# Low weight words on VectorE, and two blocks of batch 0 accumulated high words first

## The chip, the cores and the metric

The kernel runs on one core of one Trainium2 chip. The metric is the device time of one execution in microseconds (us); the profile's "span" is the part of it from the first to the last instruction. Five engines work side by side, each through its own queue in order: TensorE (PE, matrix products), VectorE (DVE), ScalarE (ACT), GpSimd (POOL) and SyncE (SP, which issues the transfers).

## The reference, cut to what matters

Four batches of 1088 tokens go through a linear attention with a quadratic feature map and then a gated feed-forward block, in which a 1088 x 1088 matrix `w_sg` mixes the tokens:

```
x   = num / den                                  # attention: per batch 1088 x 128
h   = gelu(x @ w_in)                             # 1088 x 1024
u, v = h[..., :512], h[..., 512:]
v_n = (v - mean(v)) / sqrt(var(v) + 1e-6) * g_ln # over the 512 columns
v_s = w_sg @ v_n + b_sg                          # over the tokens, per batch
out = x + (u * v_s) @ w_out
```

The mixing product is by far the largest: 1088 x 1088 x 512 in each of four batches.

## The kernel before, in words

**Two words for a number.** TensorE multiplies a reduced form of float32 (`F32R`) in one pass. To keep the precision, an operand is split into a high word (the value rounded to F32R, by a cast on ScalarE) and a low word (value minus high word, a subtraction). A product is then the sum of three: high by high, high by low, low by high. So `w_sg` is held as `w_h` (one tile, nine row blocks) and as nine tiles `w_l0` to `w_l8`; the normalized v as `vh` and `vl`.

**Tiling.** Tokens are nine row blocks (`NT`; the last has 64 rows), or three column chunks (`CH`: 364, 362, 362). The 512 columns of v and u are four blocks of 128 (`NB`, index `db`). One unit of the mixing product is a pair (`db`, `ci`): a PSUM bank `pz` of 128 x 364 takes 26 products, for each row block t `w_h` by `vh`, `w_h` by `vl` (not in the last block, whose lower half holds the low word) and `w_l` by `vh`. Names in the rows carry the batch: `pz0_1_2` is batch 0, block 1, chunk 2.

**Stages of one batch.** Attention gives x as `x_h`, `x_l`. Nine tiles `pv` (`v1`, three products each) give v before the gelu; `gelu` on ScalarE, `stats` on VectorE, then `norm`, a chain of twelve tiny VectorE instructions that gives the reciprocal root `rs` and `nm` for a group of row blocks (batch 0: blocks 0-1, 2-4, 5-8). `v3` applies them, `split_h` and `split_l` make `vh` and `vl`. `unit` (tile `pu`) makes u before its gelu (`ug`); it needs the two words of the first half of `w_in`, which VectorE converts from 64-bit floats (`wi0`, tiles `win_h`, `win_l`). `scale` and `gate` (tile `gt`) empty a `pz` bank, and three products (`po`) with `w_out` add to the output.

**What sets the order.** Each step is registered with `at(name, f)`; the table `WHEN` gives every step its rank, and the steps are issued in that order. Each engine runs its own steps in that order and waits for semaphores. PSUM has eight banks, handed out in turn: a step that takes a bank waits until its last reader is done.

**Around the change.** Batch 0 is special, since its weights have only just arrived. `w_hi` (ScalarE cast) and `w_lo` (subtraction) make the words of `w_sg`; `LO_POOL` names all nine low words, so GpSimd subtracts them. The mixing product of block 0 is done in two phases, all `w_h` products of the three chunks (`z_hi`) and then all `w_l` products (`z_lo`); blocks 1 to 3 go chunk by chunk through `main(g0, 1)`, with the three products of a row block side by side.

Of the kernel before, what the change touches and what calls it, by code (L numbers as in the profile page):

```python
# [8 lines left out]
I32 = mybir.dt.int32  # L9
# [7 lines left out]
NT = 9  # L17
# [121 lines left out]
def tile_kernel(tc, qd, kd, vd, sd, wd, bd, wind, gd, woutd, identd, outd, pool, dram, psum):  # L139
# [483 lines left out]
    def w_lo(t, E):  # L623
        T["w_l", t] = w = new([P, S], "w", f"w_l{t}", F32R)
        r = slice(0, P if t < NT - 1 else 64)
        if t == NT - 1:
            G.memset(f32(w[64:128]), 0.0)
        E.tensor_sub(w[r], T["w_f", t][r], f32(T["w_h"][r, t]))  # L628
# [350 lines left out]
```

## Time and profile before

| | |
|---|---|
| median of 3 runs | 373.79 us (373.56 to 376.94) |
| the profiled execution | 373.27 us, of which the span is 371.5 us |
| PE busy | 345.0 us, 93% of the span |
| DVE busy | 265.5 us, 71% |
| ACT busy | 165.9 us, 45% |
| POOL busy | 42.8 us, 12% |
| mean granted TensorE clock | 0.963 |

In the rows, `L628` is line 628 of the kernel as it was before; the changed kernel's lines stand one to three further. A row of the timeline gives start, duration, engine, line, operation, out<-in, shape and count, and in brackets how long the engine had been idle and what ended that. A row of the windows gives for each engine the busy us and the number of instructions in a stretch, then the granted TensorE clock, the share of the DMA engines and GB/s.

### The profile page before, as it was taken

Reading aid. Unit: us, or ns where it says so; the run is one execution under the profiler, and the core shown is the slowest. Engines: PE = TensorE matmul, PEld = TensorE weight load, DVE = VectorE, ACT = ScalarE, POOL = GpSimd, SP = SyncE. Lnnn points to the kernel's source line nnn. Section 1 sums busy time; section 2 is a strip of 40 time slices with the busy share of each in tenths; the row PEclk is TensorE's granted clock in tenths of the full one; section 3 lists DMA queues with packets and bytes.
Section 4 is the critical chain, followed back from the end, with each engine's and each line's share of the span. In section 5 each row is a group of like instructions: output and inputs, shape, how many; then the busy total and the mean of one; then the engine's idle time right before and its main releaser. Section 6 shows DMA issues by size and latency. Waiting matters only on the chain.

```text
span 371.5 us, 5469 instructions
## 1 busy us (share of the span) xinstructions
PE 345.0 (93%) x2040; PEld 329.7 (89%) x2040; DVE 265.5 (71%) x615; ACT 165.9 (45%) x361; POOL 42.8 (12%) x33
## 2 busy tenths in 40 slices
PE   8967059999989999999999999999999999999995
PEld 6866059999989999998989999999998999999994
DVE  5989997954897975655997984657999773535233
ACT  4737358524635591423565672334525861312020
POOL 0237930003200000013200000022200000000000
PEclk9969558999999999999999999999999999999999
DMA  7991020185200000176200010172000010000001
GB/s 256 377 394 60 0 84 2 26 179 164 77 0 20 2 20 23 35 159 202 50 2 20 3 40 2 38 173 66 0 2 1 2 40 2 0 20 2 0 2 60
DMA packets 13945, 24.17 MB, mean 65 GB/s; under 512 B 1856, under 2 KB 10720, under 8 KB 13920
## 3 DMA queue, kind: packets, MB, share of 16 engines
q1 hardware_dynamic: 13776, 23.75, 21.6%
q8 instruction: 16, 0.26, 0.3%
q10 hardware_dynamic: 144, 0.09, 0.1%
q14 instruction: 9, 0.07, 0.1%
HBM read 17.84 MB, written 2.65 MB: 55 GB/s over the span
## 4 chain that ended last, share of the span: by engine, by line
PE 63%; DVE 19%; DMA 8%; issue 3%; SPq 3%; ACT 2%; DVEq 0%; ACTq 0%
PE pz L725 15%; PE pz L731 15%; PE pz L727 13%; DVE den L472 3%; DMA e_2b<-e_2d 2%; SPq L434 2%; DMA e_2d<-ab 2%; PE po L794 2%; PE pu L745 2%; PE pu L746 2%; PE pu L747 2%; PE po L792 2%; PE po L793 2%; PE pv L653 2%; PE pv L655 1%
## 5 line engine op out<-in xcount | busy, mean ns | idle before, releaser
L725 PE MATMUL pz<-w_h,vh 128*128 128x362 f32 (+1 forms) x432 | 144.9, 335 | 4.1 <-ACT vh L707 3.1
L731 PE MATMUL pz<-w_l,vh 128*128 128x362 f32 (+1 forms) x432 | 137.6, 328 | 0.0
L727 PE MATMUL pz<-w_h,vl 128*128 128x362 f32 (+1 forms) x384 | 126.9, 331 | 0.0
L725 PEld LDWEIGHTS pz<-w_h,vh 128*128 128x128 f32 x432 | 82.4, 191 | 5.3 <-ACT vh L707 3.6
L731 PEld LDWEIGHTS pz<-w_l,vh 128*128 128x128 f32 x432 | 80.6, 188 | 0.0
L727 PEld LDWEIGHTS pz<-w_h,vl 128*128 128x128 f32 x384 | 73.3, 191 | 0.6 <-DVE vl L715 0.3
L757 DVE SCALAR_TENSOR_TENSOR gt<-pz,g_col,b_bc 128x362 f32<-128x362 f32 (+1 forms) x48 | 28.3, 591 | 40.2 <-PE pz L731 40.0
L768 ACT CAST gh<-gt 128x362 fp32r<-128x362 f32 (+1 forms) x47 | 23.1, 494 | 47.4 <-DVE gt L763 37.1
L752 ACT ACTIVATE u<-pu 128x362 f32<-128x362 f32 (+1 forms) x48 | 22.6, 471 | 45.9 <-PE pu L747 31.8
L771 DVE TENSOR_TENSOR gl<-gt,gh 128x362 fp32r<-128x362 f32 (+1 forms) x47 | 25.8, 552 | 12.0 <-ACT gh L768 11.2
L697 ACT ACTIVATE vn<-vn,nm,rs 128x512 f32<-128x512 f32 x36 | 27.9, 809 | 9.1 <-DVE nm L689 9.1
L707 ACT CAST vh<-vn 128x128 fp32r<-128x128 f32 (+1 forms) x72 | 25.5, 402 | 13.3 <-PE pz L731 12.9
L715 DVE TENSOR_TENSOR vl<-vn,vh 128x128 fp32r<-128x128 f32 (+2 forms) x68 | 26.0, 410 | 6.4 <-ACT vh L707 6.0
L763 DVE TENSOR_TENSOR gt<-gt,u 128x362 f32<-128x362 f32 (+1 forms) x48 | 25.5, 533 | 4.4 <-ACT u L752 3.4
L663 DVE BATCH_NORM_STATS2 st<-vn 128x6 f32<-128x512 f32 x36 | 24.4, 677 | 2.5 <-ACT vn L659 2.4
L628 POOL TENSOR_TENSOR w_l<-w_f,w_h 128x1088 fp32r<-128x1088 f32 (+1 forms) x9 | 23.2, 2574 | 24.3 <-ACT w_h L621 18.2
L659 ACT ACTIVATE vn<-pv 128x512 f32<-128x512 f32 x36 | 20.8, 599 | 10.1 <-PE pv L655 7.8
L451 POOL TENSOR_TENSOR qpl<-e_0a,qph 128x364 fp32r<-128x364 f32 x6 | 6.5, 1090 | 160.3 <-ACT qph L446 125.6
L746 PE MATMUL pu<-x_h,win_l 128*128 128x362 f32 (+1 forms) x48 | 16.6, 346 | 7.9 <-DVE win_l L230 7.9
L472 DVE RECIPROCAL den<-den 128x362 f32<-128x362 f32 (+1 forms) x9 | 21.7, 2415 | 2.2 <-ACT den L467 2.2
L745 PE MATMUL pu<-x_h,win_h 128*128 128x362 f32 (+1 forms) x48 | 16.8, 351 | 3.5 <-ACT win_h L228 3.5
L191 DVE TENSOR_TENSOR kp<-pk,kb 128x256 f32<-128x256 f32 x27 | 10.9, 420 | 8.6 <-ACT kb L354 6.3
(173 smaller groups left out, 507.7 us busy)
## 6 DMA issues: line engine op xcount, KB each, us to landing
w_f<-in_w SPq DMA_DIRECT2D x9, 544.0 KB, 8.3
vx<-in_v SPq DMA_DIRECT2D x8, 288.0 KB, 3.8
k<-in_k SPq DMA_DIRECT2D x3, 576.0 KB, 5.3
out<-o SPq DMA_DIRECT2D x7, 181.0 KB, 1.9
e_0a<-ab SPq DMA_DIRECT2D x6, 182.0 KB
e_0b<-e_0d SPq DMA_DIRECT2D x6, 182.0 KB
q<-in_q SPq DMA_DIRECT2D x6, 181.0 KB, 2.3
e_1a<-ab SPq DMA_DIRECT2D x6, 181.0 KB, 3.9
```

The source lines that it names most:

```text
L472: V.reciprocal(self.den[ci], self.den[ci])
L663: V.bn_stats(st, self.vn[:, t])
L697: A.activation(self.vn[:, t], self.vn[:, t], AF.Identity, bias=self.nm[:, t : t + 1], scale=self.rs[:, t : t + 1])
L707: A.copy(self.parts[db][0][:, ts], self.vn[:, ts, P * db : P * db + P])
L715: V.tensor_sub(vl[:, ts], vs[:, ts], f32(vh[:, ts]))
L725: mm(z, lhsT=vh[:, t], rhs=T["w_h"][:, t, cs], start=(t == 0), stop=False)
L727: mm(z, lhsT=vl[:, t], rhs=T["w_h"][:, t, cs], start=False, stop=False)
L731: mm(self.z[db, ci], lhsT=self.parts[db][0][:, t], rhs=T["w_l", t][:, c0 : c0 + cw], start=False, stop=(t == NT - 1),)
L745: mm(pu, lhsT=T["win_h"][:, ws], rhs=xh[:, cs], start=True, stop=False)
L757: V.scalar_tensor_tensor(gt, self.z.pop((db, ci)), T["g_col"][:, db : db + 1], T["b_bc"][:, c0 : c0 + cw], op0=ALU.mult, op1=ALU.add,)
L763: V.tensor_mul(self.gt[db, ci], self.gt[db, ci], self.u.pop((db, ci)))
L771: V.tensor_sub(self.g[db, ci][1], self.gt.pop((db, ci)), f32(self.g[db, ci][0]))
```

## The change

All nine low words of `w_sg` are subtracted on VectorE. In batch 0, blocks 0 and 1 (six `pz` banks) go through the two phases together: first the `w_h` products of all six, then the `w_l` products of all six. The u products (`pu`) of these blocks stand behind their `w_l` products in the list, each with its gelu. In `norm`, the shift and the multiply-add that start the reciprocal root are one instruction. And the table `WHEN` is a new one throughout, so that every engine's order differs in every batch.

```
@@ WHEN
-    0, 2, 3, 1, 4, 5, 6, 8, 12, 16, 21, 24, 27, 31, 35, 39, 44, 47, 50, 54, 59, 66, 79, 81, 34, 10, 11, 7, 13, 9,
+    0, 5, 2, 1, 3, 4, 6, 8, 12, 16, 21, 24, 26, 30, 32, 35, 40, 43, 47, 50, 54, 58, 68, 72, 41, 10, 11, 9, 13, 7,
...
-    def w_lo(t, E):
+    def w_lo(t):
...
-        E.tensor_sub(w[r], T["w_f", t][r], f32(T["w_h"][r, t]))
+        V.tensor_sub(w[r], T["w_f", t][r], f32(T["w_h"][r, t]))
...
-                lambda: V.tensor_scalar(yi(), w("v").bitcast(I32), 1, None, op0=ALU.logical_shift_right),
-                lambda: V.tensor_scalar(yi(), yi(), -1.0, float(0x9EF759DF), op0=ALU.mult, op1=ALU.add),
+                lambda: V.tensor_scalar(
+                    yi(), w("v").bitcast(I32), -0.5, float(0x1EF759DF), op0=ALU.mult, op1=ALU.add
+                ),
...
-    for ci in range(len(CH)):
-        at(("pu", 0, 0, ci), lambda ci=ci: g0.unit(0, ci))
+    def unit(g, db, ci):
+        at(("pu", g.b, db, ci), lambda: g.unit(db, ci))
+        at(("ug", g.b, db, ci), lambda: g.ug(db, ci))
+
+    for i in range(3):
+        split3(g0, 1, i)
+    for db in range(2):
+        for t in range(NT):
+            for ci in range(len(CH)):
+                at(("zh", 0, db, ci, t), lambda db=db, ci=ci, t=t: g0.z_hi(db, ci, t))
     for t in range(NT):
+        at(("wlo", t), lambda t=t: w_lo(t))
+    for db in range(2):
+        for t in range(NT):
+            for ci in range(len(CH)):
+                at(("zl", 0, db, ci, t), lambda db=db, ci=ci, t=t: g0.z_lo(db, ci, t))
         for ci in range(len(CH)):
-            at(("zh", 0, ci, t), lambda ci=ci, t=t: g0.z_hi(0, ci, t))
-    for t in range(NT):
-        at(("wlo", t), lambda t=t: w_lo(t, G if t in LO_POOL else V))
-        for ci in range(len(CH)):
-            at(("zl", 0, ci, t), lambda ci=ci, t=t: g0.z_lo(0, ci, t))
-    for ci in range(len(CH)):
-        gated(g0, 0, ci)
+            unit(g0, db, ci)
+            gated(g0, db, ci)
...
-    main(g0, 1)
+    main(g0, 2)
...
-LO_POOL = (0, 1, 2, 3, 4, 5, 6, 7, 8)
```

What the order means is seen in three places. The first is VectorE where batch 0's first norm group (tiles `nv0_0`, `ny0_0`, `nh0_0`) is worked out. Before:

```order
L680 TENSOR_SCALAR ny0_0_445<-ny0_0_445 128x2
L220 SCALAR_TENSOR_TENSOR wi0e_435<-wi0e_435,wi0g_447 128x512
L229 TENSOR_TENSOR wi0t_422<-wi0t_422,win_h_80 128x512
L681 TENSOR_TENSOR nh0_0_457<-ny0_0_445 128x2
L230 TENSOR_TENSOR win_l_82<-wi0t_422,wi0e_435 128x512
L682 TENSOR_TENSOR nh0_0_457<-nh0_0_457,nv0_0_442 128x2
```

In the changed kernel the same chain reads:

```order
L680 TENSOR_SCALAR ny0_0_406<-nv0_0_396 128x2
L664 BN_STATS st0_3_408<-vn0_143 128x6
L665 BN_AGGR mv0_364<-st0_3_408 128x2
L683 TENSOR_TENSOR nh0_0_416<-ny0_0_406 128x2
L664 BN_STATS st0_4_418<-vn0_143 128x6
L665 BN_AGGR mv0_364<-st0_4_418 128x2
L684 TENSOR_TENSOR nh0_0_416<-nh0_0_416,nv0_0_396 128x2
```

The conversion of the first half of `w_in` (`wi0t`, `wi0e`, `win_l`) no longer stands inside the chain; statistics of later row blocks (`BN_STATS`) do.

The second place is the low words. Before, they are a run on GpSimd:

```order
L628 TENSOR_TENSOR w_l3_432<-w_f3_181,w_h_79 128x1088
L628 TENSOR_TENSOR w_l4_450<-w_f4_186,w_h_79 128x1088
L628 TENSOR_TENSOR w_l6_484<-w_f6_202,w_h_79 128x1088
L628 TENSOR_TENSOR w_l7_518<-w_f7_215,w_h_79 128x1088
L627 MEMSET w_l8_566 64x1088
L628 TENSOR_TENSOR w_l8_566<-w_f8_226,w_h_79 64x1088
```

Now they stand on VectorE: two of them (`w_l1`, `w_l0`) ahead of the first `x_l`, and seven behind the last norm group, the end of which reads:

```order
L629 TENSOR_TENSOR w_l3_617<-w_f3_174,w_h_79 128x1088
L220 TENSOR_SCALAR wi0g_627<-wi0t_536 128x512
L629 TENSOR_TENSOR w_l7_631<-w_f7_199,w_h_79 128x1088
L230 TENSOR_TENSOR wi0t_536<-wi0t_536,win_h_80 128x512
L719 TENSOR_TENSOR vh0_0_458<-vn0_143,vh0_0_458 64x128
L629 TENSOR_TENSOR w_l6_647<-w_f6_192,w_h_79 128x1088
L629 TENSOR_TENSOR w_l8_656<-w_f8_209,w_h_79 64x1088
L221 SCALAR_TENSOR_TENSOR wi0e_581<-wi0e_581,wi0g_627 128x512
L231 TENSOR_TENSOR win_l_82<-wi0t_536,wi0e_581 128x512
```

The `wi0` conversion is threaded between them, and `win_l` of the first half comes last. The memset of `w_l8` is still GpSimd's; in the changed kernel that tile takes over the buffer that `w_l6` reads (`w_f6`), so the memset stands between the two subtractions.

The third place is TensorE where the mixing product of batch 0 begins. Before, behind two u tiles (`pu0_0_0`, `pu0_0_1`):

```order
L746 MATMUL pu0_0_1_476<-x0_h_333,win_l_82 128x362
L747 MATMUL pu0_0_1_476<-x0_l_334,win_h_80 128x362
L725 MATMUL pz0_0_2_507<-w_h_79,vh0_0_499 128x362
L727 MATMUL pz0_0_2_507<-w_h_79,vl0_0_500 128x362
L725 MATMUL pz0_0_1_514<-w_h_79,vh0_0_499 128x362
```

Now `pz` follows the last `pv` tile directly, and block 1 joins after twelve products:

```order
L727 MATMUL pz0_0_1_480<-w_h_79,vh0_0_458 128x362
L729 MATMUL pz0_0_1_480<-w_h_79,vl0_0_459 128x362
L727 MATMUL pz0_1_0_499<-w_h_79,vh0_1_486 128x364
L729 MATMUL pz0_1_0_499<-w_h_79,vl0_1_487 128x364
L727 MATMUL pz0_1_2_509<-w_h_79,vh0_1_486 128x362
L729 MATMUL pz0_1_2_509<-w_h_79,vl0_1_487 128x362
```

No u product stands ahead of the first `w_l` product any more: `pu0_0_0` comes behind 116 products of the mixing.

More of the change, by code (lines that the diff above doesn't have):

```diff
@@ L816, in gated @@
     def gated(g, db, ci):
-        at(("ug", g.b, db, ci), lambda: g.ug(db, ci))
         at(("gt", g.b, db, ci), lambda: g.scale(db, ci))
@@ L873, in main @@
             for ci in range(len(CH)):
-                at(("pu", g.b, db, ci), lambda db=db, ci=ci: g.unit(db, ci))
+                unit(g, db, ci)
                 for t in range(NT):
```

173 rows, old and new, of the table WHEN are left out of this document.

## The prediction

> **What bounds the kernel now.** First the busy shares, the slices and the granted clock on the page:
>
> ```profile
> PE 345.0 (93%) x2040; PEld 329.7 (89%) x2040; DVE 265.5 (71%) x615; ACT 165.9 (45%) x361; POOL 42.8 (12%) x33
> PE   8967059999989999999999999999999999999995
> POOL 0237930003200000013200000022200000000000
> PEclk9969558999999999999999999999999999999999
> ```
>
> TensorE is the bound from the seventh slice on. Before that it has a hole of three slices (9.3 us each), with the clock at half, and GpSimd is busiest just there. So the second view is the busy time by stage: the stretch and its length, then busy us and instructions of PE, PEld, DVE, ACT and POOL, the granted clock, the DMA share and GB/s:
>
> ```profile
> 35.10:52.10 17.00, 2.55 (x6) 1.69 (x6) 16.93 (x33) 7.07 (x11) 11.54 (x5) 0.59 0.09 31
> 52.10:58.70 6.60, 6.57 (x21) 6.24 (x22) 4.24 (x24) 4.13 (x8) 0.00 (x0) 0.50 0.11 40
> 58.70:110.00 51.30, 50.08 (x312) 48.44 (x311) 40.87 (x80) 25.73 (x63) 6.35 (x6) 1.00 0.33 81
> 110.00:371.50 261.50, 255.62 (x1523) 247.69 (x1522) 174.97 (x410) 110.05 (x249) 11.94 (x12) 1.00 0.13 35
> ```
>
> Between the last `pv` and the first `pz` TensorE works 2.55 of 17 us, while VectorE is full. From 58.7 on TensorE loses 1.2 us in 51, and 5.9 us in the rest, drain of the output included. The end is therefore the time at which TensorE gets going, plus a fixed amount of products. What fills VectorE in the hole is seen instruction by instruction, with GpSimd's below:
>
> ```profile
> 37.74 2.46 DVE L679 TENSOR_SCALAR ny<-nv 128x2 int32<-128x2 int32 x1
> 40.12 0.41 DVE L219 TENSOR_SCALAR wi0g<-wi0t 128x512 int32<-128x512 int32 x1
> 40.46 2.43 DVE L680 TENSOR_SCALAR ny<-ny 128x2 int32<-128x2 int32 x1
> 42.80 0.68 DVE L220 SCALAR_TENSOR_TENSOR wi0e<-wi0e,wi0g 128x512 f32<-128x512 int32 x1
> 43.41 2.96 DVE L229 TENSOR_TENSOR wi0t<-wi0t,win_h 128x512 f32<-128x512 f32 x1
> 46.40 0.69 DVE L230 TENSOR_TENSOR win_l<-wi0t,wi0e 128x512 fp32r<-128x512 f32 x1
> 47.01 2.46 DVE L682 TENSOR_TENSOR nh<-nh,nv 128x2 f32<-128x2 f32 x1
> 49.50 0.17 DVE L683 TENSOR_SCALAR np<-nh 128x2 f32<-128x2 f32 x1
> 49.58 0.17 DVE L679 TENSOR_SCALAR ny<-nv 128x3 int32<-128x3 int32 x1
> 37.60 8.21 POOL L628 TENSOR_TENSOR w_l<-w_f,w_h 128x1088 fp32r<-128x1088 f32 x3 [2.86 <-ACT w_h L621]
> 46.95 2.49 POOL L628 TENSOR_TENSOR w_l<-w_f,w_h 64x1088 fp32r<-64x1088 f32 x1
> ```
>
> A chain instruction on two columns takes 0.17 us at 49.50 and 2.46 us at 37.74. The four long ones all begin within a low word on GpSimd and end when it ends; between them one instruction of normal length slips in. They cost 4 x 2.3 = 9.1 us of this hole, and both things that TensorE waits for, `win_l` and `nm`, come out of this queue.
>
> **The change part by part.** *Head, up to the first `pv`.* The same stall stands earlier:
>
> ```profile
> 16.34 2.48 DVE L219 TENSOR_SCALAR wi1g<-wi1t 128x512 int32<-128x512 int32 x1
> 18.85 2.86 DVE L220 SCALAR_TENSOR_TENSOR wi1e<-wi1e,wi1g 128x512 f32<-128x512 int32 x1
> 25.85 0.56 DVE L602 TENSOR_TENSOR x_l<-px,x_h 128x384 fp32r<-128x384 f32 x1
> 27.94 0.48 PE L653 MATMUL pv<-win_h,x_h 128*128 128x512 f32 x1
> 34.66 0.40 PE L655 MATMUL pv<-win_l,x_h 128*128 128x512 f32 x1
> ```
>
> Against 0.41 and 0.68 us these two lose 4.2 us. That goes; two low words come in ahead of the first `x_l`. No row shows one on VectorE. Its nearest rows are subtractions of two SBUF operands on 512 columns (0.69 us, above) and on 128:
>
> ```profile
> L715 DVE TENSOR_TENSOR vl<-vn,vh 128x128 fp32r<-128x128 f32 x5 | 1.4, 283 | 1.9 <-ACT vh L707 1.9
> L628 POOL TENSOR_TENSOR w_l<-w_f,w_h x9: 2477/2552/2870, 16.0 to 46.9; 128x1088 fp32r<-128x1088 f32 x8, 64x1088 fp32r<-64x1088 f32 x1
> ```
>
> The slope is (692 - 283)/384 = 1.065 ns a column, so 1088 columns take 692 + 576 x 1.065 = 1305 ns. The lower end is 0.69 us (it cannot be shorter than a narrower one), the upper GpSimd's 2.55 us. I take 1.31 us, since it continues two rows of the same engine. The first `x_l` then starts at 25.85 - 4.2 + 2.6 = 24.2 and ends at 24.8, where `pv` can run: 3.1 us earlier than 27.94.
>
> *From `pv` to the first `pz`.* The nine `pv` tiles took 27.94 to 35.06. With the clock perhaps half for the first of them I let them end at 32.5. The last gelu and its `w_h` cast follow, then `v3`, `vh` and `pz`:
>
> ```profile
> 30.39 0.66 DVE L663 BATCH_NORM_STATS2 st<-vn 128x6 f32<-128x512 f32 x1
> 31.66 3.35 ACT L659 ACTIVATE vn<-pv 128x512 f32<-128x512 f32 x5 [0.21 <-PE pv L655]
> 35.88 0.60 ACT L659 ACTIVATE vn<-pv 128x512 f32<-128x512 f32 x1
> 50.94 0.81 ACT L697 ACTIVATE vn<-vn,nm,rs 128x512 f32<-128x512 f32 x1 [1.40 <-DVE nm L689]
> 51.78 0.30 ACT L707 CAST vh<-vn 128x128 fp32r<-128x128 f32 x1
> 52.13 0.67 PE L725 MATMUL pz<-w_h,vh 128*128 128x362 f32 x1 [3.10 <-ACT vh L707]
> ```
>
> The last gelu ended at 36.48, 1.4 us after `pv`; so now at 33.9. On VectorE, what is left ahead of `nm` of the first group is the statistics of five row blocks (0.66 us and a small second instruction, 0.8 together) and some 15 tiny instructions, 0.1 us from start to start (49.50 to 49.58). The first gelu ended at 29.6 before and would at 26.5 now; 26.5 + 5 x 0.8 + 1.5 with an `x_l` between is 32.6, and 33 with the waits for later gelus. The `wi0` conversion is gone from there. So ScalarE's gelus release `v3`, not VectorE: `pz` starts 1.19 us (50.94 to 52.13) behind 33.9, at 35.1. That is **17.0 us earlier**. One chain instruction less per group, seven in all at 0.17 us, lies beside this or beside TensorE's products later, and is costed at nothing; if VectorE were the bound there it would be worth 1.2 us.
>
> *The clock.* Products of the mixing are 0.30 us apart at half clock and 0.17 us apart at full:
>
> ```profile
> 53.22 0.51 PE L725 MATMUL pz<-w_h,vh 128*128 128x362 f32 x1
> 53.52 0.51 PE L727 MATMUL pz<-w_h,vl 128*128 128x362 f32 x1
> 59.00 0.33 PE L725 MATMUL pz<-w_h,vh 128*128 128x362 f32 x1
> 59.17 0.33 PE L727 MATMUL pz<-w_h,vl 128*128 128x362 f32 x1
> ```
>
> Before, the clock was half from 52.13 to 58.66, 6.53 us. At 58.66 TensorE had 14 `pz` and 12 `pu` products behind it. If the same 6.53 us of half clock come after 35.1, it has 21.5 products done at 41.6, and 26 at 42.4. So 58.66 corresponds to 42.4: **16.3 us**. The Trainium skill, "TensorE: Matmul & The Clock Gate", Part 1, says that the clock drops after an idle window of about 3.4 us and returns after about 3.4 us of sustained work. By it the idle stretch of 2.6 us (32.5 to 35.1) may cost no clock at all, which would speed up the phase by up to 21.5 x 0.137 = 2.9 us; the rows show 6.5 us of half clock here, longer than the page has it, and I keep to the rows in the sum.
>
> *The low phase.* Four more row blocks of statistics (3.2 us), the other two chains and six `vl` put the third group's `nm` at about 39. Seven low words stand behind it, 7 x 1.31 = 9.2 us, beside five two-operand conversions (0.69), five one-operand ones (0.41) and seven `vl` (0.28), together 7.4 us, and GpSimd's memset, for which VectorE waits between `w_l6` and `w_l8`:
>
> ```profile
> 45.87 1.00 POOL L627 MEMSET w_l<- 64x1088 f32 x1
> ```
>
> With 1.2 us for that, `w_l8` is done at about 55.5 and `win_l` at 56.8. TensorE asks for `w_l8` after 115 products: 35.1 + 6.5 + 93.5 x 0.1665 = 57.2. So VectorE's 9.2 us are covered, with 1.7 us to spare; what hides them is the doubled high phase (102 products). If a low word took 2.55 us, 7 x 1.24 = 8.7 us more would not fit, and TensorE would lose 7 us.
>
> *A wait that comes in.* Batch 1's `k` goes into the buffer that `w_l8` reads, so SP issues that load at 55.6 rather than 49.5:
>
> ```profile
> 49.47 0.33 SPq L391 DMA_DIRECT2D k<-in_k  x1
> DMA to landing us min/median/max: 5.3/5.3/5.3
> ```
>
> It lands at 61; TensorE reaches `pk1_0` at 59.5 with everything else queued behind it, and loses 1.5 us. The later `q` loads behind it on SP have time. In the stretch after it six `pz` banks are held, and two are left for `pk`, `pu`, `pab` in turn; I take the 1.2 us that TensorE loses before in 58.7 to 110 for that as well. Later batches keep their work, in another order: nothing, with 3 us either way, half of the 5.9 us that can be lost there.
>
> *The sum*, against the profiled execution (span 371.5, time 373.27): 373.27 - 16.3 + 1.5 = **358.5 us**. The median shown, 373.79, is 0.5 above that execution, which I leave inside the range.
>
> **The rivals.** *VectorE becomes the bound of the low phase* (a low word near GpSimd's price, or the long instructions have another cause than GpSimd and stay). For it: VectorE is already 16.93 of 17 us busy in the hole. Against: two-operand subtractions keep to 0.69 us elsewhere. Two low words of 2.55 us ahead of `x_l` and the 7 us above give 358.5 + 2.5 + 7 = 368.
>
> *The clock stays full* across the shorter idle stretch. The high phase is then paced by `v3` and `vh` (about 1.25 us a row block), and the low phase by `w_l8` at 55.5 instead of 57.2: 358.5 - 1.7 = 356.8, and with `pk1_0` waiting all the same, not less than 356. The 3.4 us of the Trainium skill's page on the clock gate would lead here.
>
> *The other side: too few PSUM banks.* Six of eight are held from about 40 us until the low phase ends. Behind `pk1_0` stand eight more `pk`, three `pab` and four `pu` tiles, and each takes a bank that VectorE must empty, in a queue that also holds the `wout` conversion and six `gt`. A `pk` bank costs a copy and a `kp`:
>
> ```profile
> 71.85 0.75 DVE L191 TENSOR_TENSOR kp<-pk,kb 128x256 f32<-128x256 f32 x2
> ```
>
> If each of those 15 hand-overs held TensorE for 1.2 us (one `kp` of 0.37 us, one conversion of 0.69 us ahead of it, and the signals), 18 us go: 376. It decides from 1.0 us a hand-over on (15 us). Against it: TensorE has products of three to five open `pz` units to put between, and the order does put them there.
>
> **How the numbers follow.** Forecast 0.68 (353 to 363); VectorE-bound 0.15 (364 to 371); full clock 0.12 (inside the forecast's range); PSUM 0.05 (374 to 378). The likeliest is 358.5 us. With the first and third cases and the nearer half of the second the range is 353 to 365. A measurement of this kernel tells about 1% from no change, so "same" is 370 to 377.5. Faster by over 1%: 0.68 + 0.12 + 0.14 = 0.94; the rest splits into 0.03 and 0.03.
>
> **What would show it.** Tiny chain instructions at 0.17 us everywhere before 50 us; `w_l` rows of VectorE near 1.3 us; the first `pz` at 34 to 36 us and the clock full before 43; TensorE waiting for `pk`'s load near 60. The prediction is wrong if the first `pz` comes after 40 us, if `w_l` rows are above 2 us, or if TensorE's idle time between 58 and 110 us exceeds 5 us.

## The result and the profile after

The kernel after takes **351.44 us** (median of 4 runs, 349.55 to 353.29), beside 374.9 us for the kernel before on the same chip: ratio 0.937, 95% interval 0.929 to 0.945. The profiled execution took 349.55 us with a span of 347.0 us, 23.7 us less than before. The forecast was 358.5 us with a range of 353 to 365: right in direction and in the stall that it builds on, 7 us short in size, and the median lies 1.6 us under the range. Two executions of the runs below, 380.47 us with the low words on GpSimd and 414.72 us of the kernel after, had a mean granted clock of 0.83 and 0.75 and are left out of medians and ratios.

The page of the kernel after, busy shares and slices (8.7 us each):

```profile
PE 337.1 (97%) x2040; PEld 323.2 (93%) x2040; DVE 257.3 (74%) x615; ACT 166.9 (48%) x361; POOL 19.4 (6%) x24
...
PE   8997999999999999999999999999999999999995
...
POOL 0000010023100000222000000041010000000000
PEclk9999999999999999999999999999999999999999
```

The hole of three slices in the PE row is gone, POOL is nearly empty in the head, and the granted clock is full in every slice. By stage (the columns are those of the windows in the prediction):

```profile
24.00:33.00 9.00, 6.71 (x33) 5.17 (x32) 8.67 (x40) 8.40 (x16) 0.00 (x0) 1.00 0.60 215
33.00:45.00 12.00, 12.00 (x71) 11.27 (x70) 11.69 (x35) 9.79 (x19) 0.00 (x0) 1.00 0.01 1
45.00:58.00 13.00, 12.61 (x76) 11.85 (x75) 12.76 (x21) 2.48 (x6) 1.00 (x1) 1.00 0.17 60
58.00:75.00 17.00, 17.00 (x119) 16.70 (x118) 16.27 (x36) 10.40 (x28) 1.95 (x2) 1.00 0.56 140
75.00:110.00 35.00, 34.93 (x199) 33.20 (x198) 32.83 (x72) 20.28 (x40) 3.88 (x4) 1.00 0.23 56
```

TensorE is busy from 33 us on, and VectorE is too: over 93% of every stretch up to 110 us. The instructions that were long before, and the new ones, in the timeline of VectorE; below them the last `pv` and the first `pz` on TensorE:

```profile
27.40 0.14 DVE L680 TENSOR_SCALAR ny<-nv 128x2 int32<-128x2 int32 x1
29.13 0.13 DVE L684 TENSOR_TENSOR nh<-nh,nv 128x2 f32<-128x2 f32 x1
22.45 0.55 DVE L603 TENSOR_TENSOR x_l<-px,x_h 128x384 fp32r<-128x384 f32 x1
37.60 1.29 DVE L629 TENSOR_TENSOR w_l<-w_f,w_h 128x1088 fp32r<-128x1088 f32 x1
49.03 2.61 DVE L629 TENSOR_TENSOR w_l<-w_f,w_h 128x1088 fp32r<-128x1088 f32 x2
...
29.55 0.40 PE L656 MATMUL pv<-win_l,x_h 128*128 128x512 f32 x1
31.97 0.43 PE L727 MATMUL pz<-w_h,vh 128*128 128x364 f32 x1 [2.02 <-ACT vh L709]
```

`ny` and `nh` take 0.14 and 0.13 us where they took 2.46, a low word takes 1.29 us, and the first `pz` starts at 31.97 rather than 52.13.

**Where the 24.5 us of span come from.** The first `pz` is 20.16 us earlier. Behind it, the trace is cut at the 1402nd product from the end; the stretch from there to the end of the span is, for the kernel before and the kernel after,

```profile
131.90:371.50 239.60, 233.72 (x1402) 226.93 (x1400) 156.74 (x353) 96.71 (x224) 11.94 (x12) 1.00 0.14 37
...
109.83:347.00 237.17, 232.31 (x1402) 226.40 (x1400) 155.17 (x357) 99.73 (x227) 12.26 (x12) 1.00 0.14 38
```

so 2.4 us are won in the last 1402 products and 79.8 - 77.9 = 1.9 us between the first `pz` and there.

### The profile page after: what moved, and what is told of

It reads as the page before. It is cut to its first block, busy times and chain, and to the rows that moved or that the text cites. A ratio compares the mean times of both kernels' runs of the same rounds, so it can differ in the third digit from the quotient of the medians.

```text
span 347.0 us, 5466 instructions
## 1 busy us (share of the span) xinstructions
PE 337.1 (97%) x2040; PEld 323.2 (93%) x2040; DVE 257.3 (74%) x615; ACT 166.9 (48%) x361; POOL 19.4 (6%) x24
## 4 chain that ended last, share of the span: by engine, by line
PE 65%; DVE 15%; issue 6%; DMA 6%; ACT 5%; SPq 1%; POOLq 0%; POOL 0%; ACTq 0%; DVEq 0%
PE pz L733 15%; PE pz L727 14%; PE pz L729 12%; PE pkv L370 4%; DMA e_2b<-e_2d 3%; DVE w_l L629 3%; DVE st L664 2%; PE po L796 2%; ACT vn L699 2%; PE po L794 2%; PE pu L747 2%; PE pu L749 2%; PE pu L748 2%; PE po L795 2%; PE pk L345 2%
## 5 line engine op out<-in xcount | busy, mean ns | idle before, releaser
L727 PE MATMUL pz<-w_h,vh 128*128 128x362 f32 (+1 forms) x432 | 142.2, 329 | 2.0 <-ACT vh L709 2.0
L733 PE MATMUL pz<-w_l,vh 128*128 128x362 f32 (+1 forms) x432 | 135.2, 328 | 0.0
L727 PEld LDWEIGHTS pz<-w_h,vh 128*128 128x128 f32 x432 | 81.2, 188 | 2.9 <-ACT vh L709 2.5
L729 PEld LDWEIGHTS pz<-w_h,vl 128*128 128x128 f32 x384 | 72.3, 188 | 1.4 <-DVE vl L717 1.1
L773 DVE TENSOR_TENSOR gl<-gt,gh 128x362 fp32r<-128x362 f32 (+1 forms) x47 | 25.0, 536 | 17.3 <-ACT gh L770 16.9
L709 ACT CAST vh<-vn 128x128 fp32r<-128x128 f32 (+1 forms) x72 | 25.2, 403 | 17.2 <-PE pz L733 16.7
L765 DVE TENSOR_TENSOR gt<-gt,u 128x362 f32<-128x362 f32 (+1 forms) x48 | 26.4, 551 | 1.1
L664 DVE BATCH_NORM_STATS2 st<-vn 128x6 f32<-128x512 f32 x36 | 24.5, 680 | 0.4 <-ACT vn L660 0.2
L796 PE MATMUL po<-gl,wout_h 128*128 128x362 f32 (+1 forms) x47 | 16.1, 342 | 0.2 <-DVE gl L773 0.2
L794 PE MATMUL po<-gh,wout_h 128*128 128x362 f32 (+1 forms) x47 | 15.9, 339 | 0.0
L749 PE MATMUL pu<-x_l,win_h 128*128 128x362 f32 (+1 forms) x48 | 15.8, 328 | 0.0
```

Of the source, the lines that this page charges most:

```text
L664: V.bn_stats(st, self.vn[:, t])
L709: A.copy(self.parts[db][0][:, ts], self.vn[:, ts, P * db : P * db + P])
L727: mm(z, lhsT=vh[:, t], rhs=T["w_h"][:, t, cs], start=(t == 0), stop=False)
L729: mm(z, lhsT=vl[:, t], rhs=T["w_h"][:, t, cs], start=False, stop=False)
L733: mm(self.z[db, ci], lhsT=self.parts[db][0][:, t], rhs=T["w_l", t][:, c0 : c0 + cw], start=False, stop=(t == NT - 1),)
L765: V.tensor_mul(self.gt[db, ci], self.gt[db, ci], self.u.pop((db, ci)))
```

## The experiments

### The engine alone, in the old order

The kernel before, with

```
-LO_POOL = (0, 1, 2, 3, 4, 5, 6, 7, 8)
+LO_POOL = ()
```

> The kernel before with one edit: all nine low words on VectorE, at the places that they had in the written order. Theory (the GpSimd stall is worth what VectorE loses to it, but the old order puts seven low words ahead of the first nm): the stalls of 4.2 and 9.1 us go, nothing else in the head changes kind; three low words of 1.29 us stand ahead of the first x_l and four more ahead of nm, 7 x 1.29 = 9.0 us. First pz at 52.1 - 13.3 + 9.0 = 47.8 us, total 369 us (366 to 371). Rival (the stall alone is what the change removes, and the order matters little): first pz at 39 us or earlier, total 355 to 361. Rival (no gain from the engine by itself): 372 to 375.

Measured: 370.73 us (368.73 to 371.93), ratio 0.986 (0.979 to 0.992). The first `pz` starts at 45.97, 1.8 us ahead of the theory's figure. In VectorE's timeline none of the long rows is left, and seven low words of 1.26 to 1.29 us stand ahead of the first `nm`, as expected: 9 us against the 13 at which the stall was put. Of the 6.2 us by which `pz` comes earlier, the profile loses 3.4 again before the last 1402 products. The engine by itself is a fifth of the gain.

### Order and phases alone, low words on GpSimd

The kernel after, with

```
-        V.tensor_sub(w[r], T["w_f", t][r], f32(T["w_h"][r, t]))
+        G.tensor_sub(w[r], T["w_f", t][r], f32(T["w_h"][r, t]))
```

> The kernel after with one edit: all low words back on GpSimd, order and phases as after. Theory (a VectorE instruction on two SBUF inputs, or one of the tensor-scalar kind, that starts within a low word takes until it ends): three to four such losses of about 2.2 us fall between 18 us and the first nm, two low words of 1.29 us leave VectorE there, so the first pz comes 4 to 6 us later, at 36 to 38 us; the idle stretch ahead of it grows beyond 3.4 us and the clock drops, 2 to 3 us more. Total 355 to 361. Rival (order and phases made the gain, the engine is of no matter): 349 to 352. Rival (the stall takes all of the gain): 368 or more.

Measured: 360.19 us (three runs, 359.56 to 361.14), ratio 0.958 (0.952 to 0.965), so 8 to 9 us above the kernel after. The total is where the theory put it, the first `pz` is not: 43.28 us, not 36 to 38. GpSimd's timeline, and the long rows of VectorE's:

```profile
19.12 21.32 POOL L629 TENSOR_TENSOR w_l<-w_f,w_h 128x1088 fp32r<-128x1088 f32 x8 [18.23 <-ACT w_h L622]
...
30.90 1.91 DVE L680 TENSOR_SCALAR ny<-nv 128x2 int32<-128x2 int32 x1
33.54 1.82 DVE L683 TENSOR_TENSOR nh<-ny 128x2 f32<-128x2 f32 x1
36.09 1.82 DVE L684 TENSOR_TENSOR nh<-nh,nv 128x2 f32<-128x2 f32 x1
38.02 2.45 DVE L680 TENSOR_SCALAR ny<-nv 128x3 int32<-128x3 int32 x1
```

Eight low words run back to back, and every one that meets the chain holds one tiny instruction until it ends. The stall stands in the new order just as in the old one: the mechanism of the forecast is shown from both sides. Nothing of the late `pz` comes back behind it: from there to the end of the span it is 316.1 us here and 315.1 in the first profile of the kernel after. So the total lies at the upper end of the theory's range although its delay was put too small by 5 to 7 us, and that agreement is luck in part.

### Without the two-block phases

The kernel after, with the places of TensorE's `zh` and `zl` steps filled anew; ScalarE and the loads keep their order, and so does VectorE but for one `gt` and a few `kp` and `gl` behind the low words.

```
+    fill = [all zh of block 0]
+    fill += [("zl", 0, 0, ci, t) for t in (0, 1, 2, 4, 5, 3, 7, 6, 8) for ci in range(3)]
+    for ci in (2, 1, 0):
+        fill += [(k, 0, 1, ci, t) for k in ("zh", "zl") for t in range(9)]
```

> The kernel after, its queues for VectorE, ScalarE and the loads as they are, but TensorE takes block 0's high and low products first and block 1's behind them (no two-block phases). Theory (the doubled high phase hides the low words): block 0's low products wait for low words that VectorE hands out until 51.6 us; TensorE has 81 products done at about 52.1 us, where without waiting it would have them at 31.97 + 81 x 0.167 = 45.5, so it loses 6 to 7 us, total 355 to 357. Rival (the two-block phases hide nothing, another wait sets the time): 349 to 351.

Measured: 360.86 us (359.6 to 362.29), ratio 0.959 (0.952 to 0.966): 9 us lost, 2 to 3 more than expected, and in another place. TensorE's waits between 33 and 60 us:

```profile
PE pz L771 <- ACT vh L753: 5.0, 2, 3.0
PE pz L773 <- DVE vl L761: 1.5, 2, 1.2
PE pz L771 <- DVE vh L763: 0.5, 1, 0.5
```

No wait for a low word is among them. With one block, each row block brings only six products, and TensorE runs out of row blocks before it comes to the low words. So what the doubled high phase hides here is the delivery of `vh` and `vl`, which the forecast had not said; that it hides the low words too is not shown by this run. The clock dropped twice on the way (36.25 and 46.49 us).

### The two instructions of the chain

The kernel after with the shift and the multiply-add apart again (on two chips), and the kernel before with only the one instruction.

```
-                lambda: V.tensor_scalar(yi(), w("v").bitcast(I32), -0.5, float(0x1EF759DF), op0=ALU.mult, op1=ALU.add),
+                lambda: two(),   # logical_shift_right by 1, then * -1.0 + 0x9EF759DF

-                lambda: V.tensor_scalar(yi(), w("v").bitcast(I32), 1, None, op0=ALU.logical_shift_right),
-                lambda: V.tensor_scalar(yi(), yi(), -1.0, float(0x9EF759DF), op0=ALU.mult, op1=ALU.add),
+                lambda: V.tensor_scalar(yi(), w("v").bitcast(I32), -0.5, float(0x1EF759DF), op0=ALU.mult, op1=ALU.add),
+                lambda: None,
```

> The kernel after with the shift and the affine step of the reciprocal square root as two instructions again, in the place of the one. Theory (the chain of the first group ends within 0.2 us of the last gelu, so it is nearly hidden): one or two instructions of 0.1 to 0.2 us ahead of the first nm, first pz 0.1 to 0.3 us later, total 349.7 to 350.2, not to be told from the kernel after. Rival (VectorE sets the first pz and each of the seven groups counts): 7 x 0.17 = 1.2 us, 350.7 to 351.

> The kernel after with the two instructions of the chain, once more, since its first profile had 275.1 us for the last 1601 products, where the other kernels in the new order have 272.6 to 274.4. Theory (order): 272.6 to 274.4 this time, total within 1 us of the kernel after beside it. Rival (fused instruction): 275 again, total 2 us above the kernel after.

> The kernel before, with the shift and the multiply-add of the chain as one instruction and nothing else changed. Theory (the 3 us that the later batches gain come from the new order): the last 1601 products take 275.5 to 276.3 us as before, the head gains at most one stalled instruction (2.4 us, since the two that follow each other at 37.74 and 40.46 both lasted to the end of a low word): total 371 to 373.5. Rival (the fused instruction is what the later batches gain): the last 1601 products take 273 to 274 us and the total falls by 2 to 3 us more, to 368 to 371.

Measured: two instructions in the new order 353.48 us, ratio 0.941 (0.934 to 0.947), and 355.95 us, ratio 0.947 (0.940 to 0.953), beside 352.05 and 0.938 (0.932 to 0.944) for the kernel after on the second of these chips. The intervals overlap, but both medians lie above the kernel after, by about 1 to 4 us, and the first of them above what either side expected (349.7 to 351). In both profiles the first `pz` stands 10.0 to 10.2 us behind the first `pv` rather than 9.8, 0.2 to 0.4 us against the 0.1 to 0.3 expected. One instruction in the old order gains nothing: 377.75 us, ratio 1.004 (0.998 to 1.010). The stall moves to the chain's next instructions there, in VectorE's timeline of that kernel:

```profile
44.05 2.42 DVE L683 TENSOR_TENSOR nh<-ny 128x2 f32<-128x2 f32 x1
47.65 2.47 DVE L686 TENSOR_TENSOR np<-np,nh 128x2 f32<-128x2 f32 x1
```

### The kernel after, three times more

> The kernel after, unchanged, on another chip. Theory (the clock changes only at the borders of windows of 3.41 us, and where these borders lie against the program's start differs from run to run): if the full clock comes at the first border after 4 us, the first pv starts near 22.2 us, the first pz near 32, total 349.5 to 350.5; if it comes one to three windows later, pv and pz are 2 to 3.5 us later and the total is 352 to 354; if the clock also drops for a window ahead of pz, 1.5 to 2.5 us more. Rival (the loads of the head vary in time): pv later with the clock full by 5 us.

> The kernel after, unchanged, a third time, as the measure for the kernels beside it. Its time depends on when the full clock comes in the head and on whether it drops ahead of pz: 349.5 to 350.5 with the clock full by 5 us and kept, 352 to 355 otherwise; median 350 to 354.

> The kernel after, as the measure for the two beside it: the last 1601 products take 272.5 to 273 us by the two profiles so far; total 349.5 to 355 with where the full clock comes in the head.

Measured, the second time: 353.31, 352.65 and 354.53 us, ratio 0.939 (0.934 to 0.944), without a profile of these. The third time, on the same chip: 349.61 to 354.93, median 353.37, ratio 0.935 (0.930 to 0.940); the fourth time, on another, 350.46 to 353.49, median 352.05, ratio 0.938 (0.932 to 0.944). The four ratios agree; the single times spread over 5 us. The profile of the third (352.81 us) shows one thing that separates it from the first (349.55 us). TensorE's products of `k` in the first, then in the third:

```profile
4.27 2.45 PE L503 MATMUL pk<-sk,k 128*128 128x64 f32 x18
...
4.13 4.10 PE L503 MATMUL pk<-sk,k 128*128 128x64 f32 x18
```

The same 18 products take 2.45 us at the full and 4.10 at the half clock. In the trace's clock record full clock comes at 4.19 us in the first and only at 12.73 us in the third; the first `pv` follows at 22.16 and 25.08, the first `pz` at 31.97 and 34.90. The fourth profile (351.06 us) has full clock at 3.81 and the first `pz` at 31.88. The other kernels whose head is that of the kernel after fall into the same two groups: full clock at 3.9 to 4.7 us and the first `pv` at 22.2 to 22.3, or full clock at 12.3 to 13.6 and the first `pv` at 25.1 to 25.8; one lies between (23.6), and its clock was full at 3.84 and half again from 7.25 to 10.66. So the theory on record holds for the head. It holds less for the drop ahead of `pz`, which the third profile has as well: with 1.5 to 2.5 us for it the total would be 353.5 to 356.5, and it is 352.81. And not all of the spread is the clock: the fourth profile, counted from the first `pz`, is 1.6 us behind the first from 92 us on. There TensorE waits 1.1 us for a `gl`, and VectorE, which makes it, had waited 1.1 us rather than 0.4 for a transfer (`e_2b`) at 85 us.

### The clock: filled in before, and lost in after

The kernel before, with idle products behind the last `pv`, and the kernel after, with copies ahead of the first `v3` (two, then six):

```
+        for i in range(66):
+            mm(t, lhsT=xh[:, :P], rhs=T["win_h"][:, DG:], start=True, stop=True)

+        for i in range(2):          # 6 in the second kernel
+            A.copy(T["wout_h"].rearrange("p n c -> p (n c)"), T["vn", 0][:, 0])
```

> The kernel before, with 66 idle products of 512 columns (0.23 us each, 15.2 us in all, their output is used by nobody) on TensorE behind the last pv, in the hole that it spends waiting. Theory (the clock drops since the hole leaves whole windows idle): the clock is full when pz starts at 52.1, the first 26 products take 4.3 us rather than 6.5, total 2 to 3 us below before, 370 to 372. Rival (the clock after the hole costs nothing, as VectorE paces the high phase there): 373 to 375.5, with the clock full all the same.

> The kernel after, with two copies of 128x512 on ScalarE (about 0.5 us each) ahead of the first v3; they write into a buffer that is filled later. Theory: the first pz comes 1.0 to 1.2 us later and the idle stretch ahead of it is 3.1 us, of which most falls into one window of 3.41 us in most runs, so the clock is half for one or two windows: total 1.0 plus 1.5 to 3 us above the kernel after, 352 to 354 with the early full clock, up to 357 without. Rival (an idle stretch under 3.4 us costs no clock): 1.0 to 1.2 us above.

> The same with six copies: first pz 3.0 to 3.3 us later, idle stretch 5 to 5.4 us, which leaves at least one window nearly empty whatever the grid. Theory: half clock in every run, until the end of the first window that is busy throughout, 3.4 to 6.8 us after pz's start; total 3.1 plus 1.5 to 3 us above the kernel after: 354.5 to 357 (up to 360 with a late full clock at the start). Rival (clock is of no matter, since ScalarE's v3 and vh pace the high phase at 1.1 us a row block): 3.1 us above, 352.6 to 355.

Measured: the filled hole 375.4 us (372.06 to 378.81, 10 runs), ratio 0.998 (0.994 to 1.003): no gain in the total, although the clock is full when `pz` starts. Two copies: 352.3 us, ratio 0.936 (0.930 to 0.942), not to be told from the kernel after on that chip. Its profile (352.79 us) has the early full clock, the first `pz` 1.3 us late and the clock half from 31.96 to 38.78; theory and rival both fit within the scatter of the runs, so this one decides nothing. Six copies: 357.11 us, ratio 0.948 (0.944 to 0.952), 3.4 to 3.8 us above the kernel after on that chip, with 3.9 us more of idle time (5.90 against 2.02 us) and half clock until 44.29. The rival is the nearer one there: the delay costs about its length, the half clock nothing that shows on top. The 6.5 us from the first `pz` in the kernel after and in the one with six copies, the 30 us from there in both, and then 45 us from the first `pz` in before and filled:

```profile
31.97:38.50 6.53, 6.26 (x33) 5.39 (x34) 6.19 (x28) 6.27 (x12) 0.00 (x0) 1.00 0.02 4
39.47:46.00 6.53, 6.53 (x26) 6.49 (x27) 6.02 (x25) 6.27 (x12) 0.00 (x0) 0.63 0.01 3
...
31.97:61.97 30.00, 29.34 (x174) 27.52 (x175) 29.33 (x70) 15.11 (x35) 1.00 (x1) 1.00 0.08 27
39.47:69.47 30.00, 30.00 (x173) 29.72 (x173) 28.98 (x67) 14.85 (x35) 1.00 (x1) 0.92 0.09 27
...
52.13:97.10 44.97, 44.69 (x263) 43.40 (x264) 32.84 (x86) 24.29 (x58) 4.38 (x4) 0.93 0.39 98
55.03:100.00 44.97, 44.81 (x277) 42.73 (x278) 34.95 (x85) 25.48 (x61) 4.84 (x5) 1.00 0.41 98
```

With six copies TensorE is seven products behind after 6.5 us, and one behind after 30. It is not held back by VectorE all the way: from the 15th to the 95th product from the first `pz` the kernel after has one every 0.165 us. But at the 100th the kernel with six copies is 0.9 us behind it and the third profile, with half clock for 3.41 us, 1.1; at the 130th they are 0.1 and 0.2 behind. In between the first profile waits for `win_l` and for batch 1's `k`, and the late ones find both ready. The product that reads `win_l` and the one before it, in the first profile and in the third:

```profile
52.48 0.33 PE L747 MATMUL pu<-x_h,win_h 128*128 128x364 f32 x1
53.03 0.43 PE L748 MATMUL pu<-x_h,win_l 128*128 128x364 f32 x1 [0.22 <-DVE win_l L231]
...
56.47 0.33 PE L747 MATMUL pu<-x_h,win_h 128*128 128x364 f32 x1
56.64 0.34 PE L748 MATMUL pu<-x_h,win_l 128*128 128x364 f32 x1
```

So in the new order the clock's loss falls into waits that stand there anyway. In the old order it does not: 45 us behind the first `pz` the filled hole is still 14 products ahead, 2.3 us, which is what the theory said. That its total gains nothing has other causes in its profile (375.02 us). The first `pz` comes 25.25 us behind the first `pv` rather than 24.19, in part since the idle products hold back the six `pu`, whose gelus stand ahead of the first `v3`; at 102 us TensorE waits 1.1 us for a `gl`, as in the fourth profile of the kernel after; and the first `pv` is 1.8 us later, with the full clock at 10.22 rather than 4.06. So this run does not show that the half clock is free in the old order, and its total cannot say what it costs.

### An earlier start, and no memset

The kernel after with the first group's chain ahead of the later statistics, and (apart from it, then with it) without GpSimd's memset of half of `w_l8`, whose low products then read 64 partitions.

```
+    move([("norm", 0, 0, i) for i in range(11)], ("x2", 0, 2))
+    move([("v3", 0, 0), ("vh", 0, 0, 0)], ("gelu", 0, 7))
+    move([("v3", 0, 1), ("vh", 0, 0, 1)], ("gelu", 0, 5))

-            G.memset(f32(w[64:128]), 0.0)
-                self.z[db, ci], lhsT=self.parts[db][0][:, t], rhs=T["w_l", t][:, c0 : c0 + cw], start=False,
+                self.z[db, ci], lhsT=self.parts[db][0][:r, t], rhs=T["w_l", t][:r, c0 : c0 + cw], start=False,
```

> The kernel after, with the eleven chain instructions of the first group ahead of the statistics of row blocks 2 to 8, and v3 and vh of row blocks 0 and 1 ahead of the last gelus. First pz at about 30.4 us rather than 32 (with an early full clock), idle stretch ahead of it under 0.7 us, so the clock never drops there. Theory (VectorE is full from 9 to 75 us, so products that come earlier only wait for low words and conversions): 0 to 0.7 us faster than the kernel after where the clock was kept, 1 to 2 where it had dropped. Rival (the end is the first pz plus a fixed amount of products): 1.5 us faster, and 1.5 more where the clock had dropped.

> The kernel after, without GpSimd's memset of the unused half of w_l8: the low products of the last row block read 64 partitions. VectorE no longer waits about 1 us between w_l6 and w_l8. Theory (VectorE's backlog sets the low phase): win_l 1 us earlier, total 0.5 to 1 us faster than the kernel after. Rival (TensorE is fed there anyway, it idles 0.39 us between 45 and 58 us): less than 0.4 us.

> Both edits. Theory (VectorE's backlog): the memset's 1 us lets the earlier start keep some of its lead: 1 to 1.7 us faster than the kernel after. Rival (first pz plus fixed products): 1.5 to 2.5 us. If neither is told from the kernel after, both leads end in other waits before 110 us.

Measured: the earlier start 355.01 us, ratio 0.943 (0.939 to 0.947), beside 353.37 and 0.935 for the kernel after on the same chip: no gain, rather a loss. The first `pz` did come 8.82 us behind the first `pv` rather than 9.82, and then TensorE waited for the second group of row blocks:

```profile
PE pz L747 <- ACT vh L729: 4.1, 2, 3.1
```

My reorder had put the second group's chain behind, so TensorE idled 3.1 us at 36.9, and neither theory had that: the start was not what limited it. Without the memset it is 368.68 us, ratio 0.978 (0.973 to 0.982), and 370.73 with both: a miss by 15 us, whose cause is the narrower product. From the timeline of the kernel without the memset, a product of 64 partitions among others, and its weight load:

```profile
153.84 0.41 PE L725 MATMUL pz<-w_h,vh 128*128 128x364 f32 x1
154.18 0.43 PE L732 MATMUL pz<-w_l,vh 64*128 64x364 f32 x1
154.53 0.43 PE L725 MATMUL pz<-w_h,vh 128*128 128x362 f32 x1
154.80 0.33 PE L727 MATMUL pz<-w_h,vl 128*128 128x362 f32 x1
...
154.17 0.18 PEld L732 LDWEIGHTS pz<-w_l,vh 64*128 64x128 f32 x1 [0.17 <-issue]
154.53 0.19 PEld L725 LDWEIGHTS pz<-w_h,vh 128*128 128x128 f32 x1 [0.17 <-issue]
```

Both weight loads, into the 64-row product and out of it, begin only with their own product, where they otherwise run one product ahead. From 153.84 to 154.80 three products take 0.96 us. Over the 48 narrow ones in the kernel, the products just before, of and behind a narrow one start 0.26, 0.36 and 0.27 us apart, where 0.167 is usual: 0.39 us each, 18.7 in all, of which 15 show between the medians. What the memset itself is worth stays open. No version here beats the kernel after beyond the scatter of the runs.

### The last 1402 products, in the other kernels

The expectations above speak of the last 1601 products. By that count the fourth profile of the kernel after has 274.07 us, where 272.5 to 273 was expected; the two instructions have 275.28, the rival's figure; and the one instruction in the old order has 277.34, above both sides. That stretch still holds the wait for `gl` that comes in some executions only, so the cut was moved behind it afterwards, to the 1402nd.

The same cut in the old order with VectorE's low words, in the old order with the one instruction, in the new order without two-block phases, with GpSimd's low words, and with the two instructions (second profile):

```profile
129.15:369.10 239.95, 233.90 (x1402) 227.03 (x1400) 158.18 (x353) 96.72 (x224) 11.62 (x12) 1.00 0.14 37
...
132.46:372.30 239.84, 233.79 (x1402) 226.96 (x1400) 156.31 (x349) 96.92 (x224) 11.77 (x12) 1.00 0.15 37
...
122.38:359.60 237.22, 232.29 (x1402) 226.62 (x1400) 155.43 (x357) 99.87 (x227) 12.51 (x12) 1.00 0.14 38
...
121.74:359.30 237.56, 232.45 (x1402) 226.53 (x1400) 156.43 (x357) 99.90 (x227) 12.26 (x12) 1.00 0.14 38
...
111.66:350.40 238.74, 232.97 (x1402) 226.56 (x1400) 155.97 (x362) 99.83 (x227) 12.24 (x12) 1.00 0.15 37
```

The old order takes 239.6 to 240.0 us, with one instruction or two; the new one 237.2 to 237.6 with one (the third and fourth profiles of the kernel after have 237.47 and 237.24), whichever engine has the low words and with or without two-block phases; and 238.7 and 239.1 with two. So the phases and the low words have no part in these 2.4 us. Part of the two instructions' price lies behind the last product: from its start to the end of the span it is 5.3 us with them and 4.4 to 4.8 otherwise. Up to that start it is 235.1 to 235.4 us in the old order, 233.5 to 233.8 in the new one with two instructions and 232.7 to 232.9 with one. So between the products the new order is worth 1.3 to 2.0 us and the one instruction 0.6 to 1.1, in the new order alone; the two instructions rest on two profiles. Neither theory had that both are needed. Why the end of the span is longer with two is open, as is why the old order gains nothing from one.

## Why the prediction was right in kind and short in size

By its own steps, against the first, third and fourth profile of the kernel after (349.55, 352.81 and 351.06 us):

| step (us gained) | forecast | first | third | fourth |
|---|---|---|---|---|
| first `pz` earlier by | 17.0 | 20.2 | 17.2 | 20.2 |
| from there to the last 1402 products: clock (-0.7), batch 1's `k` (-1.5) | -2.2 | 1.9 | 1.8 | 0.3 |
| last 1402 products | 0 | 2.4 | 2.1 | 2.4 |
| outside the span | 0 | -0.8 | -0.7 | -0.7 |
| sum | 14.8 | 23.7 | 20.5 | 22.2 |

Three terms of the sum failed, all to the same side: the start of the first `pz`, the clock and the load of `k` behind it, and the later batches.

*The stall* was right: 0.13 to 0.16 us for every chain instruction after, long rows again as soon as GpSimd has the low words. *The low word* was right: 1.305 us forecast, 1.28 to 1.29 measured.

*The first `pz`* was put 3.1 us too late. The profile that the forecast rests on has its full clock at 4.06 us, and like it the first and the fourth (4.19 and 3.81). That the third profile agrees to 0.2 us (34.90 against 35.1) is luck: its full clock comes at 12.73 and costs the head 2.9 us. The step that failed is the head. The first `x_l` starts at 22.45 us rather than 24.2. VectorE is busy for 18.5 us ahead of it, where the forecast's terms make 21.2 - 4.2 + 2.6 = 19.6 us, and idle for 3.9 rather than 4.6: the stall and the two low words were priced, the new order of the head was not. And the first `pv`, whose first product reads `x_h` and not `x_l`, starts 0.3 us ahead of `x_l`, where the forecast had it wait for the end of `x_l`. From the first `pv` to the first `pz` it is 9.8 us against 10.3 forecast, and the release was as forecast, by a narrow margin: ScalarE's last gelu ends at 30.86, `v3` starts at 30.77, and VectorE's `nm` is done at 30.68.

*The clock behind `pz`* was wrong twice over: half clock for 6.53 us does not carry over (none in the first and fourth profile, 3.41 us in the third), and in this order most of its price falls into waits that stand there anyway: the third profile is 1.1 us behind the first at the 100th product and 0.2 at the 130th. The full-clock rival had the clock right, and with 356.8 it was the nearer one.

*The low phase*: `w_l8` was forecast for 55.5 and TensorE's demand for 57.2. In the first profile `w_l8` was ready at 51.64, and 115 products were issued by 52.32. The cover holds, with 0.7 us to spare rather than 1.7. Behind it TensorE is held for 0.4 us by `win_l`, which is done at 52.97 rather than 56.8.

*The wait for `k`* came, but small. The load's issue on SP and the first product that reads it, in the first profile, and TensorE's wait in the fourth:

```profile
51.71 0.33 SPq L392 DMA_DIRECT2D k<-in_k  x1
...
55.47 0.41 PE L345 MATMUL pk<-sk,k 128*128 128x64 f32 x2 [0.17 <-DVE wot L218]
...
PE pk L345 <- DMA k<-in_k: 0.3, 1, 0.3
```

In the record of the load's semaphore the last part lands at 55.34 in the first profile and at 55.41 in the fourth, and the product follows 0.13 and 0.14 us later; the first row names VectorE, whose `wot` ends at the same time. Against the usual 0.167 us from product to product, TensorE loses 0.3 and 0.5 us, and nothing in the third profile, where the load is in 0.4 us ahead. What was mis-sized is the load: it takes 3.6 to 3.8 us from issue to the last part, and took 3.7 before as well (49.47 to 53.16). The 5.3 us in the forecast's row belong to a later load of `k`, issued at 79.68.

*Later batches* at nothing, 3 us either way: this term failed in every profile, by 2.1 to 2.4 us. Most of it is the new order of these batches, which was given nothing; the rest is the instruction less, which was weighed at 1.2 us and costed at nothing.

*The PSUM rival* is refuted: TensorE's idle time between 58 and 110 us is 0.07 us.

## What to carry to other kernels

When two engines share a stall, look at what the second one's work costs in the place to which it moves: the engine alone brought 5 us and order and phases alone 15, together 23. Before pricing a clock or an earlier start by the bound engine's pitch, look for the waits behind it: half clock behind the first `pz` still cost 2.3 us 45 us on in the old order, and in the new one 0.1 to 0.2 after 130 products, since waits for `win_l` and `k` took it up; and a start 1 us earlier gained nothing, since the next group came no earlier. Count products and not only totals, for a total mixes in the head's clock and transfers that vary. And an instruction less may be worth nothing in one order and about a microsecond in another: price the parts of a change together, and give a new order of everything a range of its own rather than zero.

## What the hardware showed beyond that

**The clock steps lie on a grid.** In the clock record of the kernel before, the steps come at 4.06, 21.13, 27.95, 38.19 and 58.67 us: 5, 2, 3 and 6 times 3.413 us apart. The third profile of after has them at 12.73, 36.62, 40.03 and 350.65 (7, 1 and 91 times), and the grid's offset against the program's start differs from run to run. Windows cut on the grid, of after (first profile) and of the third:

```profile
28.08:31.49 3.41, 1.86 (x9) 1.19 (x7) 3.31 (x24) 3.41 (x6) 0.00 (x0) 1.00 0.30 119
31.49:34.91 3.42, 2.67 (x13) 2.12 (x13) 3.28 (x14) 3.33 (x8) 0.00 (x0) 1.00 0.01 2
...
33.21:36.62 3.41, 1.46 (x7) 1.15 (x7) 3.27 (x16) 3.35 (x7) 0.00 (x0) 1.00 0.01 2
36.62:40.03 3.41, 3.41 (x12) 3.17 (x11) 3.17 (x17) 3.31 (x8) 0.00 (x0) 0.50 0.00 0
```

An idle stretch of 2.0 us falls across a border in the first profile (1.86 and 2.67 us busy in the two windows) and costs no clock; in the third it falls into one window (1.46 busy), and the next window runs at half clock. Half clock then lasts until about a whole window has been busy: in before the window from 51.85 with 0.28 us of idle time ahead of `pz` did not bring it back, the next one did at 58.67. So the same kernel keeps or loses its clock by where the grid lies, which is how one profile's 6.53 us misled the sum. The Trainium skill, "TensorE: Matmul & The Clock Gate", Part 1, says that the window is 3.41 us long and free-running and does not start with the kernel; these records agree. Its rule that the clock drops after an idle window does not hold to the letter: 1.95 us of idle time in a window of 3.41 were enough here, 1.55 were not. Idle time alone does not draw the line, though: with the two instructions (second profile) a window with 1.38 us, 31.22 to 34.63, lost the clock too.

**Whether narrow products count less for the clock is open.** In the third profile the windows 2.49 to 5.90 and 5.90 to 9.31 hold no idle time, but TensorE ran its first 64-column products there until 8.23, and full clock came only at 12.73, behind a window of wider ones. In the old order with VectorE's low words the window 18.39 to 21.80, in a stage of 66-column products, had 1.10 us idle and the clock dropped all the same. But in the first profile of after the window 0.78 to 4.19, with nothing but 28 products of 64 columns and 0.16 us idle, brought the full clock. This was seen, not tested.

**A product of 64 partitions among products of 128** costs about 0.39 us more, spread over itself and its two neighbours; in the rows above, its weights and those of the next product are loaded only as their own product starts.
